# Attention ahead of two MoE layers on one core: causal masks added in VectorE's maximum, softmax denominators inverted by way of DRAM, the preparation of k and q spread over two pairs

## The chip, the cores and the metric

One core of one Trainium2 chip runs the kernel. The time is the device time of one execution in microseconds (us). The engines are named as in the profile: PE (TensorE), DVE (VectorE), ACT (ScalarE), POOL (GpSimd) and SP (SyncE, which here only issues DMAs).

## What is computed

Attention with a decay and a causal mask, then a layer of eight experts mixed by a normalised gate, then one of eight experts with a single expert a row. The change touches the attention alone:

```python
B, H, S, D = 4, 8, 576, 64
scores = scale * np.matmul(q, k.transpose(0, 1, 3, 2))        # scale = 1/8
decay = cum[:, :, :, None] - cum[:, :, None, :]               # cum = cumsum(log(clip(f, 1e-4, 1)))
scores = np.where(causal, -1000000000.0, scores + decay)      # causal: column > row
scores = scores - np.max(scores, axis=-1, keepdims=True)
attn = np.exp(scores)
attn = attn / (np.sum(attn, axis=-1, keepdims=True) + 1e-09)
out = np.matmul(attn, v)
...
x = _moe_ref(x=x, **moe_kwargs)
return _moe2_ref(x=x, **moe2_kwargs)
```

## The kernel before

The 32 heads are worked off in 16 pairs, p = 0 to 15, a pair being two heads of one batch entry. Everything is float32; a number that PE multiplies at its faster rate is split into a rounded part (float32r) and its remainder, which are laid one under the other in the 128 rows of an operand. The order of every engine's instructions is the order in which the program writes them (a manual schedule): each step is a generator, and `weave` takes steps of several generators by positions between 0 and about 1 of an iteration of the main loop (lines 559 to 608). The table `SCH` (line 27) holds most positions. A pair passes through these steps, in different iterations:

- **load** (237, 240): k and q of pair p + 4 come from DRAM in two DMAs, issued by SP at the end of iteration p; v of pair p + 1 (307) right behind.
- **prep(p + 3)** (309 to 331): DMAs of the decay's row into `ka` (312) and of ones into `qb` (314), a cast of k into `ka` on DVE (318), two copies of q into `qb` (320) on ACT, two of k into `kk` (323) and two of q into `qy` (328) on ACT, and the remainders `kk` and `qy` as two subtractions of 64x1152 on POOL (325, 330). Nine steps between .2 and 1.16 of an iteration; `kk` and `qy` have four buffers each, as `ka` and `qb`.
- **path1(p + 2)** (333 to 373): the maximum of every row of scores, needed before the exponential. PE multiplies q by k in tiles of 128 rows into the two buffers `p1` of PSUM; a mask (identity times a triangle of large negative numbers, `identr` and `maskr`, 282 to 285) is added by a further matmul into the triangle of the diagonal block (344, 357, 366), seven of them a pair. DVE takes the maxima: the first two tiles hold both heads and one reduction (346) serves both; then one tile a head (358), and for the last 64 rows two reductions over 512 columns (360), a small one over the diagonal block (368), and their joining (369). Lines 371 and 372 split the negated maxima into `m20`.
- **mrow(p + 1)** (374 to 382): PE transposes `m20` (378) into a `p1` buffer, ACT copies it (380), and POOL issues the DMA that puts it into two rows of `qb` (381).
- **path2(p)** (384 to 415): scores again, transposed and with decay and maximum inside the product (389, 390), into buffers `p2`; ACT's exponential (401, 412) into `pt`; POOL sets the part above the diagonal to zero (393, 413).
- **attn_v** (417 to 464): `pt` times v, head 0 from .6 of iteration p, head 1 in iteration p + 1 (428). The v operand holds 64 columns of v and 64 of ones, so that 64 rows of the result carry the denominators. ACT reads result and denominators apart, two instructions of 64x576 a head (461, 462).
- **norm** (466 to 482): six reciprocals of 128x96 (471) and one product of 128x576 (474) on DVE, and the store to `xgd` (480), over iterations p + 1 and p + 2.
- **norm_few** (484 to 507) takes the place of norm for p = 13 and p = 15 (`FEW`, 510): ACT reads result and denominators together (452), a DMA lays the 1152 denominators out as 32x36 (453), DVE takes one reciprocal of them (488), a DMA writes them to DRAM (489), two DMAs read them back, each to 64 partitions (493), two products of 64x576 (497) and two to four stores (505) follow.

The MoE stages take the rest of the span; weights and x for them are fetched and prepared from p = 8 on.

## Time and profile before

| | |
|---|---|
| three runs, us | 2044.25, 2044.49, 2046.55 (median 2044.49) |
| the profiled execution, us | 2045.49 |
| its span, us | 2043.8 |
| busy over the span: PE, DVE, ACT, POOL | 98%, 78%, 41%, 12% |
| granted TensorE clock (mean) | .999 |
| instructions | 28069 |

The span is that of the instructions that the profiler recorded; the execution's own time is 1.69 us longer. A busy share over the whole span says little about the attention stage, which is a ninth of it: the views of single stretches and the timelines are the ones to read. PE's matmuls overlap and their ends are modelled, so the time from one start to the next tells what one takes from its stream.

### The profile page before, as it was taken

What the parts mean: (1) busy time and instruction counts of PE and PEld (TensorE: products, weight loads), DVE (VectorE), ACT (ScalarE), POOL (GpSimd) and SP (SyncE); (2) the same over time, 40 slices, a digit from 0 to 9 for tenths busy, and PEclk for the clock granted to TensorE, in tenths of its full rate; (3) what the DMA queues carried; (4) which work ended last, traced back from release to release, by engine and by line L of the source; (5) the groups of instructions that cost most, each with busy time, mean ns of one, the idle gap of its engine ahead of it and who ended that gap; (6) DMA issues with size and microseconds to landing.
All of it is one profiled execution on the core that took longest, in us unless ns stands there. A gap on an engine that the chain in (4) does not pass through costs nothing. (4 is left out here: it accounts for less than half of the span.)

```text
span 2043.8 us, 28069 instructions
## 1 busy us (share of the span) xinstructions
PE 1999.7 (98%) x10257; PEld 1774.6 (87%) x10257; DVE 1594.8 (78%) x3023; ACT 834.4 (41%) x1415; POOL 243.5 (12%) x302
## 2 busy tenths in 40 slices
PE   5999999999999999999999999999999999999998
PEld 4998878889989988998998898889989998888887
DVE  8999888887777787888888788888888876555625
ACT  4888543333333343333333334333333332344524
POOL 6776200000000010000001001000000100022111
PEclk9999999999999999999999999999999999999999
DMA  4555331122113123212222223222112223155424
GB/s 148 177 174 209 111 130 62 62 67 78 62 62 114 62 85 104 88 68 73 78 77 63 93 85 109 79 68 93 68 68 82 69 63 114 68 196 176 157 84 151
DMA packets 58483, 203.01 MB, mean 99 GB/s; under 512 B 20578, under 2 KB 24486, under 8 KB 41948
## 3 DMA queue, kind: packets, MB, share of 16 engines
q1 hardware_dynamic: 53152, 189.52, 27.4%
q0 software_dynamic: 4992, 11.29, 1.6%
q8 instruction: 82, 1.34, 0.3%
q14 instruction: 69, 0.57, 0.1%
q10 hardware_dynamic: 188, 0.28, 0.1%
HBM read 185.93 MB, written 15.86 MB: 99 GB/s over the span
## 5 line engine op out<-in xcount | busy, mean ns | idle before, releaser
L964 PE MATMUL o<-w,H 128*128 128x512 f32 x1152 | 450.3, 391 | 0.0
L962 PE MATMUL o<-w,H 128*128 128x512 f32 x1152 | 450.1, 391 | 0.0
L963 PE MATMUL o<-w,H 128*128 128x512 f32 x1152 | 450.0, 391 | 0.0
L1016 ACT ACTIVATE H<-u 128x384 fp32r<-128x384 f32 x192 | 101.0, 526 | 630.6 <-DVE u L1031 624.3
L964 PEld LDWEIGHTS o<-w,H 128*128 128x128 f32 x1152 | 216.2, 188 | 45.5
L962 PEld LDWEIGHTS o<-w,H 128*128 128x128 f32 x1152 | 216.3, 188 | 42.7
L963 PEld LDWEIGHTS o<-w,H 128*128 128x128 f32 x1152 | 216.2, 188 | 42.2
L995 DVE SCALAR_TENSOR_TENSOR acc<-o,Pt,acc 128x512 f32<-128x512 f32 x252 | 188.4, 748 | 75.3 <-PE o L964 73.8
L943 PE MATMUL C<-xc,wc 128*128 128x384 f32 x1152 | 234.0, 338 | 1.5 <-DVE c L1078 1.3
L943 PE MATMUL B<-xc,wc 128*128 128x384 f32 x1152 | 231.8, 335 | 2.4 <-DVE u L1063 1.4
L943 PE MATMUL A<-xc,wc 128*128 128x384 f32 x1152 | 231.9, 335 | 1.2
L943 PEld LDWEIGHTS C<-xc,wc 128*128 128x128 f32 x1152 | 204.4, 188 | 11.4 <-DVE c L1078 2.1
L943 PEld LDWEIGHTS A<-xc,wc 128*128 128x128 f32 x1152 | 201.9, 188 | 4.6 <-ACT ta L1059 4.5
L943 PEld LDWEIGHTS B<-xc,wc 128*128 128x128 f32 x1152 | 202.1, 188 | 4.1 <-DVE u L1063 2.3
L1020 DVE SCALAR_TENSOR_TENSOR H<-A,H 128x384 fp32r<-128x384 f32 x96 | 53.5, 557 | 108.0 <-ACT H L1016 108.0
L219 DVE TENSOR_TENSOR w<-raw,w 128x512 fp32r<-128x512 f32 x190 | 123.6, 683 | 0.4 <-ACT w L215 0.4
L193 DVE TENSOR_TENSOR wc<-tw,wc 128x512 fp32r<-128x512 f32 x188 | 123.7, 694 | 0.0
L1016 ACT ACTIVATE H<-c 128x384 fp32r<-128x384 f32 x96 | 50.5, 526 | 178.9 <-DVE c L1078 178.9
L943 PE MATMUL D<-xc,wc 128*128 128x384 f32 x576 | 116.0, 335 | 1.0 <-DVE wc L193 1.0
L428 PE MATMUL av<-pt,va 128*128 128x192 f32 (+3 forms) x448 | 109.9, 359 | 1.6 <-DMA va<-in_va_dram 1.6
L1020 DVE SCALAR_TENSOR_TENSOR H<-u,H 128x384 fp32r<-128x384 f32 x192 | 109.9, 572 | 1.3 <-ACT H L1016 1.2
L869 POOL DMA_INDIRECT slots<-pay,sli x18 | 19.4, 1078 | 720.4 <-DVE base L867 357.4
(330 smaller groups left out, 3418.5 us busy)
## 6 DMA issues: line engine op xcount, KB each, us to landing
raw<-in_wa_dram SPq DMA_DIRECT2D x95, 1024.0 KB
kq<-in_kq_dram SPq DMA_DIRECT2D x32, 576.0 KB
raw<-in_wb_dram SPq DMA_DIRECT2D x16, 1024.0 KB
wc<-in_wb_dram SPq DMA_DIRECT2D x16, 1024.0 KB
va<-in_va_dram SPq DMA_DIRECT2D x16, 640.0 KB
xr<-xgd SPq DMA_DIRECT2D x21, 384.0 KB
x1d<-acc SPq DMA_DIRECT2D x18, 256.0 KB
wgb<-in_wg2t_dram SPq DMA_DIRECT2D x16, 256.0 KB
```

Source lines behind the costliest of these rows:

```text
L193: eng.tensor_tensor(wc[:, 1, c], src, wc[:, 0, c].bitcast(F32), op=ALU.subtract)
L219: nc.vector.tensor_tensor(t[:, 1, c], raw[:, c], t[:, 0, c].bitcast(F32), op=ALU.subtract)
L428: PE.matmul(av[:, 256 + i0:256 + i1], vt[:, jt, h, :], rhs, start=start, stop=stop)
L869: POOL.indirect_dma_start(out=slot_list[t % 4], in_=pay[:, t, :], in_offset=None, out_offset=bass.IndirectOffsetOnAxis(ap=sli[:, t:t + 1], ...
L943: PE.matmul(a[:, 0:L], w[wa_][k], x[:, xa_, k], start=(start and k == i == 0), stop=(stop and k == 1 and i == 2), skip_group_check=True)
L962: PE.matmul(o, h[:, 0, ts_], w[:, 0, c], start=(b == 0), stop=False)
L963: PE.matmul(o, h[:, 0, ts_], w[:, 1, c], start=False, stop=False)
L964: PE.matmul(o, h[:, 1, ts_], w[:, 0, c], start=False, stop=(b == 3))
L995: DVE.scalar_tensor_tensor(ac, o, p[e], ac, op0=ALU.mult, op1=ALU.add)
L1016: ACT.activation(h[f_][:, 0, half * L:(half + 1) * L], src, AF.Relu)
L1020: DVE.scalar_tensor_tensor(h[f_][:, 1, c], src, 0.0, h[f_][:, 0, c].bitcast(F32), op0=ALU.max, op1=ALU.subtract)
```

## The change

**Masks.** The seven mask matmuls go, and `identr` and `maskr` with them. A tile `mask` in SBUF holds 384 columns of zeros and then the triangle (128 columns); a slice of it is added in the same DVE instruction that takes the maximum (sum and maximum, in place on PSUM, with an accumulator that a second instruction reads out). Each such maximum covers one head, so there are ten a pair in place of eight reductions and a joining; the last two take the maximum over the 512 columns before as their start.

**Denominators.** `norm_few` serves every pair but p = 14. A pair's reciprocal and write stand at the start of iteration p + 2, the broadcasts near its .38, the products and stores from .66. The broadcast of a head goes into the half of the other head's result tile that holds spent denominators. `rx`, `r`, `x` and `den` have three buffers; the DRAM tiles are 16.

**Preparation and loads.** `prep(p + 3)` makes its first two steps (the cast, the copies to `qb`, the DMAs) between .5 and .8 of iteration p, and its other seven (copies to `kk` and `qy`, POOL's subtractions) between .02 and .75 of iteration p + 1. `kk` and `qy` have three buffers instead of four. The load of k and q stands at .82 to .88 in the iteration, that of v at .64 to .7.

```diff
-        kk_, qy_ = (... bufs=NQ) for _ in range(NQ)] ...)
+        kk_, qy_ = (... bufs=NK) for _ in range(NK)] ...)
...
+            def top(out, src, rows, m, first=LOWEST):
+                DVE.tensor_tensor_reduce(src, src, mask[0:rows, m], 1.0, first, ALU.add, ALU.max, out)
...
                 for h in range(2):
-                    PE.matmul(a3[:, h], qb_[:, h, n - P:n], ka_[:, h, 0:n], start=(h == 0), stop=False, ...)
-                PE.matmul(a3[:, :, n - P:n], identr, maskr.unsqueeze(1).to_broadcast([P, 2, P]), ...)
-                DVE.tensor_reduce(mx.rearrange("p (h i) -> p h i", h=2)[:, :, it], a3, axis=AX.X, op=ALU.max)
+                    PE.matmul(a3[:, h], qb_[:, h, n - P:n], ka_[:, h, 0:n], start=(h == 0), stop=(h == 1), ...)
+                for h in range(2):
+                    top(mx[:, 5 * h + it:5 * h + it + 1], a3[:, h], P, slice(512 - n, 512))
...
                     if it < 4:
-                        PE.matmul(a[:, i0:jl], identr, maskr, start=False, stop=True)
-                        DVE.tensor_reduce(mx[:, col:col + 1], a[:, :jl], axis=AX.X, op=ALU.max)
+                        top(mx[:, col:col + 1], a[:, :jl], P, slice(512 - jl, 512))
...
-            PE.matmul(a[:, 0:128].rearrange(...), identr, maskr[:, 0:64].unsqueeze(1).to_broadcast([P, 2, 64]), ...)
-            DVE.tensor_reduce(mo[:, 2:4], a[:64, 0:128].rearrange("p (h j) -> p h j", h=2), axis=AX.X, op=ALU.max)
-            DVE.tensor_tensor(mx[0:64].rearrange("p (h i) -> p h i", h=2)[:, :, 4], mo[:, 0:2], mo[:, 2:4], op=ALU.max)
+            for h in range(2):
+                top(mx[0:64, 5 * h + 4:5 * h + 5], a[:64, 64 * h:64 * h + 64], 64, slice(384, 448), mo[:, h:h + 1])
...
-            r = mo.rx[:, 2 * S:3 * S] if p == npair - 1 else mo.rk[:, 0]
+            r = [t[f"x{1 - h}"] for h in range(2)]
...
-        FEW = (npair - 3, npair - 1)
+        FEW = [p for p in range(npair) if p != npair - 2]
...
+            elif p > 1:
+                items += [(norms[p - 2], 1, 0.02, 0.08), (norms[p - 2], 1, 0.35, 0.41), (norms.pop(p - 2), 3, 0.66, 0.9)]
...
+            if p + 4 < npair:
+                items.append((iter_kq(p + 4), 1, 0.82, 0.88))
+            if p + 1 < npair:
+                items.append((iter_v(p + 1), 1, 0.64, 0.7))
...
+            if p and p + 2 < npair:
+                items.append((late, 7, 0.02, 0.75))
             if p + 3 < npair:
-                items.append((prep(p + 3), 9, *(SCH["pr"] if p else (0.5, 1.0))))
+                late = prep(p + 3)
+                items.append((late, 2, 0.5, 0.8))
             weave(*items)
-            if p + 4 < npair:
-                load(p + 4)
-            if p + 1 < npair:
-                load_v(p + 1)
```

How the order of instructions moves, at two places. First DVE where a pair's row maxima have just been split and the next pair's begin (`p_...` are PSUM tiles, `mx_...` the maxima, `m_...` the split ones). Before:

```order
L371 TENSOR_SCALAR m_1160<-mx_119 128x10
L372 SCALAR_TENSOR_TENSOR m_1160<-mx_119,m_1160 128x10
L471 RECIPROCAL r<-r 128x96 x2
L346 TENSOR_REDUCE mx_118<-p_1177 128x2
L346 TENSOR_REDUCE mx_118<-p_1193 128x2
L318 CAST ka_113<-kq 64x2x576
L358 TENSOR_REDUCE mx_118<-p_1210 128x1
L358 TENSOR_REDUCE mx_118<-p_1228 128x1
```

Now:

```order
L371 TENSOR_SCALAR m_845<-mx_131 128x10
L372 SCALAR_TENSOR_TENSOR m_845<-mx_131,m_845 128x10
L488 RECIPROCAL den<-den 32x36
L341 ISA p_856,mx_130<-p_856,mask 128x128
L341 ISA mx_130 128x1
L341 ISA p_856,mx_130<-p_856,mask 128x128
L341 ISA mx_130 128x1
L341 ISA p_873,mx_130<-p_873,mask 128x256
L341 ISA mx_130 128x1
L341 ISA p_873,mx_130<-p_873,mask 128x256
L341 ISA mx_130 128x1
L341 ISA p_887,mx_130<-p_887,mask 128x384
```

Two reciprocals of 128x96 ahead of the maxima have become one of 32x36, the two double maxima have become four with a read behind each, and the cast has gone from behind them.

Second, PE at the same place, from the second tile of a pair's row maxima to the transposition of the pair before (L378). Before:

```order
L343 MATMUL p_897<-ka_114,qb_110 128x256 x2
L344 MATMUL p_897<-maskr,identr 128x2x128
L389 MATMUL p_906<-qy,kk 128x320
L390 MATMUL p_906<-qb_108,ka_112 128x320
L389 MATMUL p_906<-qy,kk 128x192
L390 MATMUL p_906<-qb_108,ka_112 128x192
L428 MATMUL av_876<-pt,va 128x192
L355 MATMUL p_914<-ka_114,qb_110 128x384
L357 MATMUL p_914<-maskr,identr 128x128
L378 MATMUL p_918<-cs,m_864 20x128
L389 MATMUL p_923<-qy,kk 128x192
L390 MATMUL p_923<-qb_108,ka_112 128x192
```

Now:

```order
L348 MATMUL p_873<-ka_126,qb_122 128x256 x2
L389 MATMUL p_878<-qy,kk 128x320
L390 MATMUL p_878<-qb_120,ka_124 128x320
L389 MATMUL p_878<-qy,kk 128x192
L390 MATMUL p_878<-qb_120,ka_124 128x192
L428 MATMUL av_848<-pt,va 128x192
L358 MATMUL p_887<-ka_126,qb_122 128x384
L378 MATMUL p_890<-cs,m_845 20x128
L389 MATMUL p_895<-qy,kk 128x192
```

The two mask matmuls are gone from the stretch (L344, L357); the transposition follows the third tile's product directly, in the buffer that the second tile held.

## Rows read from the trace of the kernel before

**Rows 1.** Busy time by stretch: start:end, length, PE, PEld, DVE, ACT, POOL, PEclk, DMA, GB/s.

```profile
43.05:57.36 14.31, 14.31 (x88) 13.27 (x88) 12.00 (x18) 10.18 (x18) 11.99 (x14) 1.00 0.54 180
57.36:69.28 11.92, 11.92 (x82) 11.01 (x82) 10.38 (x19) 10.43 (x18) 9.30 (x15) 1.00 0.42 154
119.67:131.59 11.92, 11.92 (x82) 11.01 (x80) 11.23 (x21) 10.44 (x19) 8.78 (x12) 1.00 0.52 184
176.00:204.00 28.00, 26.70 (x177) 23.95 (x176) 25.31 (x47) 22.82 (x40) 19.30 (x29) 1.00 0.49 169
```

**Rows 2.** Timeline of PE at a pair's start: start, length, line, operation.

```profile
124.25 0.33 PE L344 MATMUL p<-maskr,identr 128*128 128x256 f32 x1
124.42 0.28 PE L389 MATMUL p<-qy,kk 128*128 128x256 f32 x1
...
125.31 0.53 PE L343 MATMUL p<-ka,qb 128*128 128x256 f32 x2
125.68 0.28 PE L344 MATMUL p<-maskr,identr 128*128 128x256 f32 x1
125.80 0.30 PE L389 MATMUL p<-qy,kk 128*128 128x320 f32 x1
...
126.81 0.22 PE L357 MATMUL p<-maskr,identr 128*128 128x128 f32 x1
126.87 0.27 PE L378 MATMUL p<-cs,m 128*20 128x128 f32 x1
```

**Rows 3.** DVE's groups, attention stage (34 to 236): busy us, mean ns | idle before.

```profile
L471 DVE RECIPROCAL r<-r 128x96 f32<-128x96 f32 x84 | 59.5, 726 | 0.0
...
L358 DVE TENSOR_REDUCE mx<-p 128x1 f32<-128x512 f32 x30 | 19.5, 651 | 1.4 <-PE p L357 1.4
...
L358 DVE TENSOR_REDUCE mx<-p 128x1 f32<-128x384 f32 x29 | 14.8, 540 | 0.8 <-PE p L357 0.7
...
L474 DVE TENSOR_TENSOR x<-x,r 128x576 f32<-128x576 f32 x13 | 9.0, 690 | 0.0
```

**Rows 4.** Timeline of DVE, same pair.

```profile
123.26 0.22 DVE L368 TENSOR_REDUCE mo<-p 64x2 f32<-64x128 f32 x1
123.51 0.63 DVE L369 TENSOR_TENSOR mx<-mo 64x2 f32<-64x2 f32 x1
...
125.75 0.95 DVE L346 TENSOR_REDUCE mx<-p 128x2 f32<-128x256 f32 x2
126.62 1.51 DVE L318 CAST ka<-kq 64x1152 fp32r<-64x1152 f32 x1
```

**Rows 5.** Timeline of POOL, same pair.

```profile
121.49 2.64 POOL L325 TENSOR_TENSOR kk<-kq,kk 64x1152 fp32r<-64x1152 f32 x1
...
124.87 2.65 POOL L330 TENSOR_TENSOR qy<-kq,qy 64x1152 fp32r<-64x1152 f32 x1 [0.36 <-ACT qy L328]
```

**Rows 6.** DVE's groups over the whole run.

```profile
L801 DVE CUSTOM_DVE_ANT_0 dump<-acc,wgb 128x512 f32<-128x512 f32 x96 | 65.6, 684 | 6.1 <-DMA wgb<-in_wg2t_dram 6.1
...
L1031 DVE TENSOR_TENSOR u<-C,u 128x384 f32<-128x384 f32 x96 | 53.2, 554 | 19.5 <-PE C L943 19.4
...
L801 DVE DVE_READ_ACCUMULATOR2_ANT lg<- 128x1 f32 x96 | 7.9, 83 | 0.0
```

**Rows 7.** Single lines: shortest/median/longest ns, first and last start us.

```profile
L318 DVE CAST ka<-kq x16: 751/1511/4043, 14.8 to 187.3; 64x1152 fp32r<-64x1152 f32 x16
...
L369 DVE TENSOR_TENSOR mx<-mo x16: 153/636/1530, 29.5 to 209.4; 64x2 f32<-64x2 f32 x16
...
L488 DVE RECIPROCAL den<-den x1: 357/357/357, 221.2 to 221.2; 32x36 f32<-32x36 f32 x1
...
L493 SPq DMA_DIRECT2D kq<-rden x2: 488/538/589, 222.9 to 223.5; - x2
...
L497 DVE TENSOR_TENSOR r<-r,kq x1: 840/840/840, 227.4 to 227.4; 64x576 f32<-64x576 f32 x1
```

More of the change, by code (lines that the diff above doesn't have):

```diff
@@ L64, in tile_attn_moe_moe2 @@
     xgd = [dram.tile([KD, P, TG * P], F32, name=f"xgd{g}") for g in range(NG)]
-    rd = [dram.tile([2, S], F32, name=f"rden{i}") for i in range(2)]
+    rd = [dram.tile([2, S], F32, name=f"rden{i}") for i in range(B * NP)]
     sm = ctx.enter_context(tc.tile_pool(name="sm", bufs=1))
@@ L241, in load_kq @@
             return t
-        kk_, qy_ = ([sb.tile([P, 2, w], F32R, name=n, bufs=NQ) for _ in range(NQ)] for n, w in (("kk", SI), ("qy", S)))
+        kk_, qy_ = ([sb.tile([P, 2, w], F32R, name=n, bufs=NK) for _ in range(NK)] for n, w in (("kk", SI), ("qy", S)))
         qb = [sb.tile([P, 2, SI], F32R, name=f"qb_{i}", tag=f"qb_{i}", bufs=1) for i in range(NQ)]
@@ L265, in clear @@
                 POOL.memset(t[0:64, :, S:SI].bitcast(F32), 0.0)
-            POOL.memset(kk_[i][:, :, S:SI].bitcast(F32), 0.0)
+            if i < NK:
+                POOL.memset(kk_[i][:, :, S:SI].bitcast(F32), 0.0)
         pattern(POOL, one[:, 0:1280], 4)
@@ L281, in attention @@
             POOL.memset(p4_[i], 0.0)
-        identr = sb.tile([P, P], F32R, name="identr", bufs=1)
-        POOL.tensor_copy(identr, ident)
-        maskr = sb.tile([P, P], F32R, name="maskr", bufs=1)
-        POOL.tensor_copy(maskr, cmask)
+        mask = sb.tile([P, 512], F32, name="mask", bufs=1)
+        POOL.memset(mask[:, 0:384], 0.0)
+        POOL.tensor_copy(mask[:, 384:512], cmask)
         clear(1)
@@ L456, in attn_v @@
             if h == 0:
-                t["r"] = sb.tile([P, S], F32, name="r", bufs=2)
-                t["x"] = sb.tile([P, S], F32, name="x", bufs=2)
+                t["r"] = sb.tile([P, S], F32, name="r", bufs=3)
+                t["x"] = sb.tile([P, S], F32, name="x", bufs=3)
             o = slice(64 * h, 64 * h + 64)
@@ L486, in norm_few @@
             b, hp = divmod(p, NP)
-            u = FEW.index(p)
+            u = p
             DVE.reciprocal(t["den"], t["den"])
@@ L496, in norm_few @@
                 o = slice(64 * h, 64 * h + 64)
-                DVE.tensor_tensor(t[f"x{h}"][o], t[f"x{h}"][o], r[o], op=ALU.mult)
+                DVE.tensor_tensor(t[f"x{h}"][o], t[f"x{h}"][o], r[h][o], op=ALU.mult)
                 yield
@@ L518, in first_weights, with iter_kq, iter_v @@
             yield from mo.sums_w(0, r, tmp, wc, DVE)
+        def iter_kq(p):
+            load(p)
+            yield
+        def iter_v(p):
+            load_v(p)
+            yield
         def chain(*gens):
@@ L588, in attention @@
             if p == npair - 2:
-                mo.rk = sb.tile([P, 1, S], F32, name="kq", bufs=2)
                 items.append((fw, 3, *SCH["w0"]))
```

46 lines of the change are left out of this document (21 added, 25 removed).

## The prediction, made before the changed kernel had run

> **What bounds the kernel now.** I read first how long each engine is busy in single stretches [rows 1]. The change touches only the attention stage, about the first 236 us of the span; it goes through 16 pairs of heads, and in each pair PE multiplies, ACT takes exponentials, DVE takes maxima and divides, POOL cuts triangles and subtracts. Two stretches that are one pair long each, 62 us apart, both last 11.92 us. DVE is busy 10.38 us in the one and 11.23 in the other, POOL 9.30 and 8.78; PE is busy all 11.92 in both. A period that stays the same while DVE's sum moves by .85 us isn't DVE's, though DVE has little room. So in the middle pairs **PE sets the period**, and an edit is worth what it takes off PE's stream, so long as nobody makes PE wait. The first pair (14.31 us) and the stretch from 176 to 204 us are different: PE still fills the first, but POOL has 11.99 us of work there, and later PE is idle 1.3 us of 28.
>
> Then PE's timeline [rows 2], where starts tell more than durations, since matmuls overlap: from a mask matmul's start to the next start is what it takes from the stream. Then DVE's groups and timeline [rows 3, 4] beside POOL's [rows 5], for what DVE must do more, and when.
>
> **1. The mask matmuls go.** By starts [rows 2]: the two of 256 columns take .17 (124.25 to 124.42) and .12 us (125.68 to 125.80), each of four of 128 columns .06 (126.81 to 126.87), and the one at a pair's end, of 128 columns in two pieces, I put at no more than .12. The sum is .29 + .24 + .12 = .65; the stream won't close up quite without a gap, so I take **.6 us a pair**.
>
> **2. DVE: what it gets and loses.** Lost for a pair [rows 3, 4]: six reciprocals (6 x .726 = 4.36), their product (.69), the two double maxima (.95), two maxima of 512 and two of 384 columns (1.30 + 1.08), the small maximum (.22) and its joining (.63): 9.2, and about 8.4 once the overlaps of neighbours come off. Gained: ten masked maxima. The trace has no such instruction on PSUM; the nearest rows [rows 6] are the 128x512 custom product with its accumulator read (.684 + .083), and a 128x384 sum of a PSUM and an SBUF tile (.554). The line through the two gives .42 for 256 columns, .29 for 128 and .23 for 64, so twice (.68 + .55 + .42 + .29 + .23) = 4.35, less ten overlaps of .08: 3.55. Ten reads add 0 to 1.6 (.8 taken, at .083), and second maxima of a shared tile that wait for the first some .4. One small reciprocal (.36) [rows 7] and two products of 64 rows (.75 each taken, between the .84 of the one shown [rows 7] and the .69 of 128 rows [rows 3]) make it **6.6**; the ends are 5.4 (no reads, no waits) and 7.9 (reads of .16 and twice the waits). DVE's work falls by 1.8 at the likeliest, .5 at the worst. As PE sets the period this is worth nothing by itself; it is what keeps the dearer maxima off the path. The cover gone, each .1 us of DVE above PE's period would cost 1.3 us in all.
>
> **3. What is given back.** The place is the start of a pair, where PE's transposition of the maxima (L378) takes the p1 buffer that the second tile before it held. In the timeline the two double maxima run from 125.75 to 126.70 [rows 4], and the transposition starts at 126.87 [rows 2]: .17 of slack. The masked maxima of those two tiles are four instructions instead of two: 2 x (.29 + .083) less an overlap = .67 for the first tile, 2 x (.42 + .083) less one = .93 for the second. Count in today's times, with the masks ahead of it (.17 + .12 + .06) gone: the transposition is due at 126.52, and the second tile's matmuls, which end at 125.84 now, at 125.67. If DVE comes to that tile at once, .93 later is 126.6, a wait of .1; if it starts on the two tiles as late as today, at 125.75 + .67 + .93 less an overlap = 127.27, a wait of .75. DVE has less to do ahead of it, so it will come earlier, but not by all of that: I take **.3 a pair**, with .1 and .75 as ends.
>
> The Trainium skill ("VectorE: DVE Perf Modes", section "The DRAIN you can't avoid") says that an operation doesn't start until the one before has left the pipeline, and so speaks against splitting one maximum into two. The trace shows some overlap: the pair of maxima runs to 126.70 and the cast after it starts at 126.62. By the rule alone four maxima would hold the tile some .3 longer, the whole .6 would go back, and the sum would be no change.
>
> **4. POOL's subtractions and DVE.** A DVE operation with two SBUF operands, or a cast, waits until a POOL subtraction has ended: the tiny joining of 64x2 started at 123.51 and ended at 124.14, when the subtraction begun at 121.49 ended (124.13); its shortest run is .153 [rows 4, 5, 7]. The cast begun at 126.62 ended at 128.13, behind the subtraction that ends at 127.52, against .751 at its shortest. A maximum with one operand, inside the first subtraction, took its usual .22. Two products of 64 rows now stand where one stood, and POOL subtracts in .44 of a pair's time (2 x 2.65 of 11.92): the pair's stall there lies between 0 and 2.65; by the change's positions they fall into the later subtraction, so 2.0 is taken. So DVE has 11.23 less stalls of .48 and .76 = 10.0 of its own now, 8.2 after, and with the cast's stall (.6) and the products' (2.0) 10.8: under PE's 11.3 (11.92 - .6). Hidden, but barely.
>
> **5. The denominators' way.** Reciprocal, write, two broadcasts and 2 to 4 half stores a pair on SP. The one pair that does it now has the reciprocal at 221.2, broadcasts issued at 222.9 and 223.5, and the products at 227.4 [rows 7]; that is 4.5 us from first broadcast to product, waits and order included. The change leaves from .38 to .7 of a period, 3.8 us, and DVE must wait if the data is late, with the maxima queued behind. Between no wait and .7 us a pair I take none: that pair's products weren't shown to wait for the transfer. One ACT read of 128 rows replaces two of 64: less work on an engine that has 1.5 us to spare [rows 1]. Moving the casts and copies over two pairs and the loads ahead by a fifth of a period changes no count; POOL keeps the same two subtractions. I cost these at nothing, PE's full stream being the cover. The last two pairs keep their way.
>
> **6. The start.** The first 20 maxima stand ahead of PE in the first pairs without cover: +1.2 to +1.6 us. Against that the first pair's stretch is freed of two POOL subtractions' share and four ACT copies that move a pair later: -1 to -2. Net 0, ends -2 and +2.
>
> **The sum.** (.6 - .3) x 13 pairs in the middle = -3.9 us; start and end 0. The profiled execution took 2045.49 us (span 2043.8), 1.0 above the median of the runs, 2044.49; taken off the median the forecast is **2040.6 us**, on its own terms 2037 to 2043.5 (.5 to .1 us a pair, with a part of the start's ends).
>
> **The rivals.**
> *All of PE's gain stays* and more: the maxima come early, the period falls to 11.3 (-7.8), the start gives 1.2 and the late pairs, where PE is idle 1.3 us [rows 1], another 1.5 of DVE's relief: 2034. For it: DVE's falling sum. Against: the .17 of slack at the transposition.
> *All given back*: the wait there is .6 to .75 a pair (0 to +2 in all) and the start dear by up to 1.5: 2045 to 2047, taken as 2046, no change (2043 to 2049). For it: DVE has no idle time ahead of those two maxima [rows 4]; it comes to them late, behind reciprocals.
> *Slower, the masked maxima are held by POOL as the joining was.* They read the mask from SBUF. Then DVE's held kind is maxima 4.7 + products 1.5 + cast .75 = 7.0, to be laid end to end with POOL's 5.3 [rows 5]: 12.3, or 13.3 where half of DVE's other 2 us falls outside; 12.8 is .9 over today, 11.7 in all: 2056 (2050 to 2063). It decides once DVE's sum passes 11.92. Against: the other operand is in PSUM, and a maximum of one PSUM operand ran freely [rows 4].
> The Trainium skill ("SBUF — State Buffer", section "Who interferes with whom") says that a vector operation with at most one SBUF input doesn't contend with GpSimd, and one with two does; the trace agrees for the .22 maximum and for the joining, and no row has a PSUM and an SBUF input beside a subtraction. By it this rival falls away.
> *Slower, the broadcasts come late*: .5 us of DVE wait over its spare .6 in most pairs, +6: 2050. Transfers are busy half the time [rows 1], and a kq load now starts nearer to them.
> *The change doesn't do what it says* only in that p = 14 keeps its reciprocals; this moves nothing.
>
> **How the numbers follow.** Forecast .38, all kept .24, all given back .23, held by POOL .10, late broadcasts .05. 0.2% is 4.1 us: faster means under 2040.4, slower over 2048.6. Faster: half of the forecast's own range lies there (.19), and all of "all kept" (.24): .43. Slower: the held maxima .10, the broadcasts .05, and a quarter of "given back" .06: .21. Same: .36. The range from 2032 to 2050 takes in the first three cases with their ends and leaves out the held maxima and part of the broadcasts and of the best.
>
> **What would show it.** The pair's period, first: near 11.6, with PE still busy in all of it. The transposition waiting for DVE's second maxima by some .3. The 128x512 masked maximum near .68 with a read of about .08; if it is twice that where POOL subtracts, the POOL rival is right. Products longer than .75 beside a subtraction. DVE's sum per pair near 10.8; if it falls to 9 and the period to 11.3, all is kept. A period unchanged at 11.9 with PE idle at one place a pair is the second rival; DVE idle in front of the products on a transfer is the fourth. I am wrong if the period moves while PE's work does not, that is if PE was not the bound.

## The result, and the profile after

The changed kernel is slower: the median of its four runs is 2057.16 us (2053.16 to 2059.17) against 2044.37 before, a ratio of 1.0059 with a 95% interval of 1.0040 to 1.0078. The forecast was 2040.6 us, its range 2032 to 2050: the time is 16.6 over the forecast and outside the range. The profiled execution took 2053.16 us with a span of 2051.5, 7.7 more than before's 2043.8.

```profile
PE 1997.4 (97%) x10145; PEld 1760.9 (86%) x10145; DVE 1572.1 (77%) x3163; ACT 812.4 (40%) x1389; POOL 254.3 (12%) x301
```

The page's busy times don't tell where the loss is. The starts of the transposition L378 do: there is one a pair, and from one to the next is a pair's **period**. Number the 15 periods of the attention stage from the first. From the PE timelines of before and after, in us:

```
                before   after
first L378       30.15   24.31
periods 1 to 2   25.20   24.04
period 3         11.91   11.43
periods 4 to 11  95.36   99.75   (11.92 and 12.47 each in the mean)
period 12        11.93   16.23
period 13        13.05   16.71
period 14        13.05   16.54
period 15        10.99   12.36
rest of span   1832.16 1830.13
```

So the start gave 5.84 us and the end 2.03, periods 1 to 3 another 1.64; periods 4 to 11 took 4.39, and the last four 12.82 (4.30, 3.66, 3.49, 1.37). The sum is +7.7. The medians differ by 12.8; the profiled execution is the fastest of its four, and the rest isn't in these periods. In a second profile of the same program (e18 below, 2057.23 us, near the median) the first transposition starts 3.96 later and periods 4 to 11 are the same 12.46, so some 4 us of the rest lie in the start.

The busy times by stretch, whose columns are those of [rows 1], for periods 3, 5, 12 and 13:

```profile
48.35:59.78 11.43, 11.33 (x74) 10.11 (x75) 7.65 (x27) 8.69 (x17) 8.44 (x12) 1.00 0.41 139
72.62:85.08 12.46, 11.84 (x73) 10.12 (x74) 10.27 (x29) 8.68 (x16) 9.25 (x13) 1.00 0.62 191
159.53:175.76 16.23, 12.79 (x74) 11.13 (x75) 8.83 (x28) 8.68 (x16) 8.28 (x12) 0.91 0.69 243
175.76:192.47 16.71, 13.58 (x74) 11.71 (x73) 12.34 (x30) 9.28 (x17) 9.31 (x12) 0.88 0.59 199
```

In period 3 no products are due yet, and PE's stream without masks takes 11.43 us, .49 less than before. From period 4 on it is 12.46: PE is idle .6 us, though DVE has only 10.27 us of work. Period 12 is 4.8 longer than period 3 and DVE has *less* to do in it than in period 5: something is waited for.

DVE's groups of the attention stage (34 to 246 us); they answer to [rows 3, 6, 7]:

```profile
L341 DVE CUSTOM_DVE_ANT_0 p<-p,mask 128x512 f32<-128x512 f32 x28 | 19.4, 692 | 4.2 <-PE p L358 4.1
...
L497 DVE TENSOR_TENSOR r<-r,x 64x576 f32<-64x576 f32 x14 | 18.6, 1326 | 10.5 <-DMA x<-rden 9.2 <-DMA r<-rden 1.2
L341 DVE CUSTOM_DVE_ANT_0 p<-p,mask 128x384 f32<-128x384 f32 x28 | 16.0, 576 | 13.4 <-PE p L358 13.4
L341 DVE DVE_READ_ACCUMULATOR2_ANT mx<- 128x1 f32 x112 | 15.6, 139 | 0.0
...
L115 DVE TENSOR_TENSOR xc<-xr,xc 128x768 fp32r<-128x768 f32 x7 | 11.5, 1642 | 7.0 <-ACT xc L114 6.9
...
L497 DVE TENSOR_TENSOR x<-x,r 64x576 f32<-64x576 f32 x14 | 10.6, 756 | 0.4
```

The masked maxima cost what was taken for them (.692 and .576 against .68 and .55), the reads .139 instead of .083. But the first of the two products takes 1326 ns in the mean where the second, of the same size, takes 756, and DVE stands 10.5 us ahead of it for the broadcasts. The remainder of x (L115) takes 1642 in the mean.

DVE's timeline in period 5 (start, length, line, operation, idle time before):

```profile
74.17 0.57 DVE L341 CUSTOM_DVE_ANT_0 p<-p,mask 128x384 f32<-128x384 f32 x1 [1.09 <-PE p L358]
...
75.07 0.70 DVE L341 CUSTOM_DVE_ANT_0 p<-p,mask 128x512 f32<-128x512 f32 x1 [0.27 <-PE p L358]
...
77.70 0.68 DVE L362 TENSOR_REDUCE mo<-p 64x1 f32<-64x512 f32 x1 [0.49 <-PE p L358]
78.31 2.11 DVE L497 TENSOR_TENSOR r<-r,x 64x576 f32<-64x576 f32 x1
80.35 0.67 DVE L362 TENSOR_REDUCE mo<-p 64x1 f32<-64x512 f32 x1
81.06 0.76 DVE L497 TENSOR_TENSOR x<-x,r 64x576 f32<-64x576 f32 x1
81.85 0.28 DVE L341 CUSTOM_DVE_ANT_0 p<-p,mask,mo 64x64 f32<-64x64 f32 x1
...
82.64 0.17 DVE L371 TENSOR_SCALAR m<-mx 128x10 fp32r<-128x10 f32 x1
...
83.37 0.30 DVE L341 CUSTOM_DVE_ANT_0 p<-p,mask 128x128 f32<-128x128 f32 x1
...
84.53 0.43 DVE L341 CUSTOM_DVE_ANT_0 p<-p,mask 128x256 f32<-128x256 f32 x1
84.88 0.14 DVE L341 DVE_READ_ACCUMULATOR2_ANT mx<- 128x1 f32 x1
```

POOL's timeline, same pair, and then PE's:

```profile
72.42 2.65 POOL L326 TENSOR_TENSOR kk<-kq,kk 64x1152 fp32r<-64x1152 f32 x1
...
77.18 2.63 POOL L331 TENSOR_TENSOR qy<-kq,qy 64x1152 fp32r<-64x1152 f32 x1
```

```profile
85.08 0.28 PE L378 MATMUL p<-cs,m 128*20 128x128 f32 x1 [0.47 <-DVE mx L341]
```

The product begun at 78.31 ends at 80.42, .6 after the subtraction of 77.18 (79.81), nearly as if it had begun there: it is **held**. A masked maximum at 74.17, inside the subtraction of 72.42, took its usual .57. DVE waits for PE three times before the hold (1.09, .27, .49) and never after it: the last maxima, the scaling into `m20`, and the first four maxima of the next pair run back to back until the transposition, which waits .47. A product free of the hold takes about .74, so this one is 1.37 late, and the period is 1.03 over 11.43; in period 4 the hold is 2.57, 1.83 over, and the period 1.41 over. About .4 us a pair is **slack** (time that a delay may take without making the pair longer), the rest is paid.

The last pairs differ. SP's queue (start, length of the issuing, transfer), DVE, POOL and PE there:

```profile
158.74 4.24 SPq L102 DMA_DIRECT2D xr<-xgd  x4
163.03 0.43 SPq L489 DMA_DIRECT2D rden<-den  x1
167.28 0.48 SPq L493 DMA_DIRECT2D x<-rden  x1
```

```profile
170.19 0.75 DVE L497 TENSOR_TENSOR r<-r,x 64x576 f32<-64x576 f32 x1 [4.90 <-DMA x<-rden]
...
180.79 3.27 DVE L115 TENSOR_TENSOR xc<-xr,xc 128x768 fp32r<-128x768 f32 x1 [1.52 <-ACT xc L114]
```

```profile
180.61 2.64 POOL L331 TENSOR_TENSOR qy<-kq,qy 64x1152 fp32r<-64x1152 f32 x1
```

```profile
171.81 0.41 PE L348 MATMUL p<-ka,qb 128*128 128x128 f32 x2 [3.44 <-DMA qb<-slots]
```

In period 12 SP issues four loads of x in 4.24 us, then the write of the reciprocals, and the broadcasts 4.25 us behind the write, once that has landed; the product stands 4.90 us for them. The 4.25 is not peculiar to this pair, for from write to broadcast the other middle pairs take 1.5 to 5.1; what is peculiar is that the write is issued 5.1 us after its reciprocal has ended (157.93), behind the loads. Behind the broadcasts in the same queue is the row of ones for `qb`, and PE waits 3.44 for that. Without the row of ones PE would have begun hardly earlier: the buffer of its tile comes free only at 171.55, when the maximum behind the late product has ended. What follows shows in the busy times of the end of period 12 and the start of 13:

```profile
168.37:171.81 3.44, 0.00 (x1) 0.03 (x1) 1.58 (x3) 0.00 (x0) 0.00 (x0) 1.00 0.38 107
171.81:175.76 3.95, 3.95 (x20) 3.52 (x21) 3.33 (x16) 1.76 (x3) 0.65 (x3) 0.65 0.87 317
175.76:182.00 6.24, 6.24 (x40) 5.75 (x39) 3.22 (x7) 5.37 (x11) 5.80 (x8) 0.95 0.42 146
```

After PE has done nothing for 3.44 us its granted clock is .65 (part of the time at 1.2 GHz) for the next 3.95 us, and near full again after that. The idle time and .35 of 3.95 make 4.82, and period 12 is 4.80 over 11.43. In period 13 the remainder of x starts .18 us after a subtraction and takes 3.27 (.95 unheld); in period 14 another takes 3.44.

Three theories were put to the test, two out of these lines and one (B) my own term of the transposition's buffer. **A, held by POOL**: an operation of DVE with two SBUF operands (product, remainder of x) stands behind a subtraction on the stretch from the last tile to the next transposition, where no slack is. **B, the buffer**: four maxima instead of two keep the `p1` tile from the transposition. **C, late broadcasts**: SP's order delays the reciprocals' way.

### The profile page after: what moved, and what is told of

Same layout as the page of the kernel before. It is cut to its first block, busy times and chain, and to the rows that moved or that the text cites. A ratio compares the mean times of both kernels' runs of the same rounds, so it can differ in the third digit from the quotient of the medians.

```text
span 2051.5 us, 28162 instructions
## 1 busy us (share of the span) xinstructions
PE 1997.4 (97%) x10145; PEld 1760.9 (86%) x10145; DVE 1572.1 (77%) x3163; ACT 812.4 (40%) x1389; POOL 254.3 (12%) x301
## 5 line engine op out<-in xcount | busy, mean ns | idle before, releaser
L955 PEld LDWEIGHTS C<-xc,wc 128*128 128x128 f32 x1152 | 204.4, 188 | 11.3 <-DVE c L1090 2.1
```

Source lines behind the costliest of these rows:

```text
L955: PE.matmul(a[:, 0:L], w[wa_][k], x[:, xa_, k], start=(start and k == i == 0), stop=(stop and k == 1 and i == 2), skip_group_check=True)
```

## The experiments

Where the expectations speak of "pair 10" and the two after it, periods 12, 13 and 14 are meant.

What all of them gave: the median of 5 to 12 runs in us (4 for before and changed) and the 95% interval of the ratio to before's runs on the same chip beside it; then from each one's profile the start of the first transposition, the mean of periods 4 to 11, and the last four:

```
                          median   ratio             first  4 to 11  period 12  13    14    15
before                    2044.37                    30.15  11.92    11.93 13.05 13.05 10.99
changed                   2057.16  1.0040 to 1.0078  24.31  12.47    16.23 16.71 16.54 12.36
e18 changed, once more    2058.20  1.0052 to 1.0079  28.27  12.46    15.24 17.69 15.27 12.94
e6  no subtractions       2040.11  .9966 to .9985    23.58  11.83    16.98 12.93 12.71 12.76
e7  masks only            2044.82  .9993 to 1.0011   30.66  12.42    12.19 13.75 13.59 10.55
e3  masks back on PE      2063.08  1.0077 to 1.0104  27.86  12.55    18.82 16.59 16.65 12.81
e5  products later        2053.51  1.0031 to 1.0065  24.31  12.37    18.45 16.61 16.48 10.98
e1  subtractions earlier  2057.46  1.0047 to 1.0075  30.52  12.95    15.48 14.95 14.28 13.89
e17 transposition apart   2056.52  1.0048 to 1.0081  24.26  12.49    17.88 16.15 16.56 12.65
e2  x loaded later        2060.71  1.0066 to 1.0094  28.17  12.47    17.20 16.79 16.54 12.35
e14 reciprocal earlier    2056.73  1.0048 to 1.0072  30.48  12.44    17.69 16.52 16.57 12.52
e11 broadcasts by ACT     2076.67  1.0142 to 1.0170  28.16  13.80    14.69 21.62 17.03 12.35
e8  three moves           2048.59  1.0000 to 1.0021  30.49  12.44    16.07 13.04 12.19 11.69
e9  five moves            2052.02  1.0020 to 1.0038  24.60  12.81    14.11 14.12 12.06 13.75
e10 five, start too       2051.01  1.0015 to 1.0035  25.32  12.89    12.71 16.50 12.56 12.80
e12 five, by ACT          2078.10  1.0128 to 1.0161  30.44  13.83    16.65 15.97 15.37 13.48
e13 halves                2053.01  1.0023 to 1.0050  28.16  12.44    16.38 14.67 14.10 12.08
e15 e13, e14, x spread    2043.63  .9984 to 1.0002   28.16  12.13    12.11 12.44 12.24 14.34
e16 e15, other order      2036.36  .9945 to .9970    25.04  12.04    11.44 12.70 12.71 12.87
```

**e18** is the changed kernel unaltered.

> The changed kernel unaltered, once more: its middle periods again 12.3 to 12.5, pair 10 16 us, the next two 16 to 17, by all theories; the first transposition somewhere between 24 and 31 us, and the time between 2053 and 2060 with it.

The first transposition comes anywhere from 23.6 to 30.7 us, 24.31 and 28.27 in two executions of the changed kernel itself. Single times differ by as much, so the periods say more than one time. The last pairs differ too. Period 14 of changed, then of e18:

```profile
192.47:209.01 16.54, 13.23 (x73) 11.44 (x74) 12.39 (x30) 9.30 (x18) 9.37 (x12) 0.90 0.32 87
```

```profile
196.68:211.95 15.27, 11.61 (x73) 10.12 (x73) 12.23 (x30) 9.32 (x18) 9.65 (x13) 1.00 0.29 82
```

PE waits 3.21 us in the one and 3.22 in the other, behind a remainder of x that is held for 3.44 in both. The granted clock is .90 and 1.00. So of the 3.49 by which period 14 is over before's, some 1.3 are the clock and 2.2 the hold.

**e6, no subtractions**: POOL's two instructions are dropped from the changed kernel, so the remainders of k and q stay the rounded copies.

```
-            POOL.tensor_tensor(kk[64:128, :, 0:S], ...)
-            POOL.tensor_tensor(qy[0:64], ...)
```

> The changed kernel without POOL's two subtractions of 64x1152 a pair, so that the remainders of k and q stay the rounded copies (part of the computation left out); nothing else is moved. Theory A: no DVE operation is held, the product takes .75 us, the two x remainders near 1 us, middle periods 11.4 to 11.7. Theory B: middle periods stay at 12.2 or more. Theory C: as pairs get faster the broadcasts (some 7.5 us from reciprocal to product) set them instead: DVE waits on the transfer in front of the product and the periods lie between 11.6 and 12.2, irregular; pair 10 keeps its 16 us.

```profile
68.03:79.48 11.45, 11.33 (x73) 10.12 (x74) 8.98 (x29) 8.70 (x17) 3.11 (x10) 1.00 0.60 207
```

Period 5 (the columns of the stretches above) falls to 11.45, DVE's sum from 10.27 to 8.98, the products take .75, and the transposition doesn't wait, with all of the masked maxima still there. Periods 13 and 14 fall from 16.6 to 12.8. Period 12 stays at 16.98, and of the middle ones those are long (up to 12.51) in which DVE waits for a broadcast (up to 1.40). So the subtractions are what the middle and periods 13 and 14 pay for, as A says, and C holds for period 12.

**e7, masks only**: before, with the changed kernel's masked maxima (and, for room, its list of zeros laid in the mask's own zeros).

```
-                PE.matmul(a3[:, :, n - P:n], identr, maskr...)
-                DVE.tensor_reduce(mx...[:, :, it], a3, axis=AX.X, op=ALU.max)
+                for h in range(2):
+                    top(mx[:, 5 * h + it:5 * h + it + 1], a3[:, h], P, slice(512 - n, 512))
```

> The kernel before with the masked maxima alone: no mask matmuls, reciprocals and preparation as before. DVE loses 3.7 us of maxima a pair and gains 5.4 (ten at 3.5, ten reads at .14, four waits at .1): 12.9 busy against PE's 11.3 and today's period of 11.92. If masked maxima need the denominators' change as cover: middle periods 12.7 to 13.2, 10 to 17 us slower than before. If the masked maxima fit into DVE's slack: 11.9 or less and no slower.

No difference that can be told. Most middle periods are 12.19 here, with DVE busy 11.35 to 11.63 us, and the transposition waits .46 or .47: with six reciprocals a pair DVE comes late, and PE's .49 is given back and .3 more, though no large operation is held there. This profile was the slowest of its ten runs (2050.21); what made the median no worse than before's is open. Much worse was expected: that was a miss.

**e3, masks back on PE** (`identr` and `maskr` and the seven mask matmuls as before), the rest changed.

> The changed kernel with the mask matmuls and the plain maxima of before, all else of the change kept. Theory B (masked maxima are what costs): the wait at the transposition goes, the middle pairs fall from 12.42 to 11.9 us (PE's stream with masks), 4 to 6 us faster. Theory A: DVE has about 1 us less to do a pair, but the product stays held for 2 us and PE gets .6 us more a pair; the middle pairs stay between 12.2 and 12.8 us and the time within 4 us of the changed kernel.

Period 5, and in it DVE's product:

```profile
76.91:88.88 11.97, 11.97 (x83) 10.94 (x81) 9.34 (x16) 8.90 (x17) 8.93 (x12) 1.00 0.63 210
```

```profile
82.95 2.38 DVE L499 TENSOR_TENSOR r<-r,x 64x576 f32<-64x576 f32 x1
```

Periods 4 to 7 are 11.96 to 11.99, nearly before's 11.92, and theory A had expected 12.2 to 12.8: a miss. The product is held here too, 1.6 us, and PE is never idle. PE's stream is .5 longer with the masks, and ahead of the transposition stand two maxima instead of four, so the delay still fits. The hold costs a middle pair something only together with the masked maxima, and e6 shows the converse: four maxima without a hold cost nothing. From period 8 on it is 12.6 to 13.7, where DVE waits 2.0 to 3.3 ahead of the product, in two of four for a broadcast by the profile, and period 12 is 18.82. So the other half of the change does harm without the masks' help, through C from period 8 on and, in periods 13 and 14, through a held remainder of x (3.26) and a held cast (3.18).

**e5, products later; e1, subtractions earlier.**

```
e5 -(norms.pop(p - 2), 3, 0.66, 0.9)   +(norms.pop(p - 2), 3, 0.84, 1.08)
e1 -(late, 7, 0.02, 0.75)              +(late, 7, 0.02, 0.52)
```

> The changed kernel with the products and their stores at .84 to 1.08 of an iteration instead of .66 to .9: behind POOL's second subtraction, and with 2 us more for the broadcasts. Periods are from one transposition (L378) to the next, since the start itself differs by up to 6 us between runs. Theory A (a DVE operation held by a subtraction sends its delay round a loop of DVE's maxima, PE, ACT and POOL): product near .75 us, middle periods 11.4 to 11.8 instead of 12.3 to 12.5. Theory B (the transposition's buffer): still 12.2 or more, with the wait of .47 in front of L378. Theory C (late broadcasts): the 4.9 us wait in pair 10 shrinks by 2 us or more.

> The changed kernel with the other seven steps of the preparation between .02 and .52 of an iteration instead of .02 and .75, so that POOL's second subtraction begins some 1.7 us earlier, ahead of DVE's products. Theory A (the products of two SBUF operands, and the x remainder of 128x768 in two late pairs, are held by that subtraction, and the maxima queued behind them come late): the first product falls from 2.1 to 2.6 us to about .75, the middle pairs from 12.42 to 11.9 us or less (4 us or more over eight pairs), the two x remainders from 3.3 us to about 1 (4 to 5 us more): 8 us faster than the changed kernel. Theory B (four masked maxima instead of two hold the PSUM buffer that the transposition wants, .47 us a pair): products fall too, but the middle pairs stay at 12.3 to 12.5 and the time within 5 us. Theory C (broadcasts late behind other loads): the 4.9 us wait in pair 10 stays.

Later products make most middle periods 12.2 instead of 12.4; theory A had expected 11.4 to 11.8, another miss. In a period of 12.19, DVE's two products and then PE's transposition:

```profile
93.07 0.74 DVE L497 TENSOR_TENSOR r<-r,x 64x576 f32<-64x576 f32 x1
93.84 0.76 DVE L497 TENSOR_TENSOR x<-x,r 64x576 f32<-64x576 f32 x1
```

```profile
96.60 0.28 PE L378 MATMUL p<-cs,m 128*20 128x128 f32 x1 [0.46 <-DVE mx L341]
```

Nothing is held on the stretch, but the products now stand behind the scaling into `m20`, after DVE's last wait for PE, and the pair is .76 over 11.43. So what decides is what stands on that stretch, held or not.

Earlier subtractions make them 12.95, dearer than changed. DVE's timeline of e1, then POOL's:

```profile
109.14 3.52 DVE L319 CAST ka<-kq 64x1152 fp32r<-64x1152 f32 x1
...
113.80 0.74 DVE L497 TENSOR_TENSOR r<-r,x 64x576 f32<-64x576 f32 x1
```

```profile
109.38 2.66 POOL L331 TENSOR_TENSOR qy<-kq,qy 64x1152 fp32r<-64x1152 f32 x1
```

The product is free, and the cast is held in its place: 3.52 where .75 is its length. It starts .24 us ahead of the subtraction, and is held all the same, while the subtraction takes its usual 2.66. A hold that is moved isn't removed.

**e17, transposition apart**: it takes a tile of `p2` instead of `p1`, for B.

```
-            a = ps.tile([P, 512], F32, name="p1", bufs=2)
+            a = ps.tile([P, 512], F32, name="p2", bufs=2)
```

> The changed kernel with one edit: the transposition of the maxima takes a PSUM buffer of path2's pair (p2) instead of one of path1's (p1), so that it no longer waits for the maxima of the tile two before. Theory B: the .47 us wait at L378 and the .7 us before its weights go, and with them .4 us or more of each middle period: 12.42 falls to 12.0 or less, 4 us faster over all. Theory A: the wait is only where DVE's delay by the hold is paid; it moves to the next matmul that needs a p1 buffer, and the middle periods stay within .15 us of 12.42.

The wait of .47 is gone, .16 stands ahead of a score tile instead, the middle periods are 12.2 to 12.6 but for one of 13.47, and the time doesn't move. The buffer is where the delay shows, not where it comes from.

**e2, x loaded later** (`mo.load_x(0, 0)` at .42 of its iteration instead of at its start); **e14, reciprocal earlier** (it and its write at .8 of iteration p + 1, the broadcasts at .1 of the next: `+(norms[p - 1], 1, 0.8, 0.81)`).

> The changed kernel with the four loads of x (1.5 MB) in iteration 10 issued at .43 of it, behind the broadcasts, instead of at its start. Theory C (the denominators' write stands behind 4.2 us of issues of those loads and behind their data): DVE's wait of 4.9 us ahead of pair 10's product vanishes, the period of 16.2 us there falls to about 12.4, and the time by about 4 us. Theory A and B: if DVE waited for something else there, the period stays at 16 us and the time unchanged.

> The changed kernel with the denominators' chain begun a quarter of an iteration earlier: reciprocal and write at .8 of the iteration before, ahead of the load of k and q on SP's queue, broadcasts at .1, products where they were. Theory C by itself: DVE's waits for broadcasts (10.4 us) go, pair 10 falls from 16.2 to 13 or less; middle periods stay at 12.2 to 12.5 since POOL still holds the product (theory A), the next two pairs at 16 to 17. About 4 us faster. If pair 10 stays above 15 us, the transfers of the preparation, not the denominators', make it late.

Neither cures C alone. In e2 PE waits 3.52 for the row of ones instead; in e14 the product waits 5.77, since the four loads of x still stand ahead of the broadcasts in SP's queue.

**The write and the broadcasts issued by ACT**, alone (**e11**), and with the moves of e9 (**e12**).

```
-            SP.dma_start(rd[u]...)
+            (ACT if p < npair - 2 else SP).dma_start(rd[u]...)
```

> The changed kernel with one edit: the denominators' write and the two broadcasts of pairs 0 to 13 are issued on ACT's DMA queue instead of SP's, so that they don't stand behind the loads of k, q, v and x on one queue. Theory C (the transfer's way through SP's queue is late in pair 10): write to broadcast takes 2 us or less instead of 3.5 to 4.2, DVE's wait of 4.9 us in pair 10 goes, its period falls from 16.2 to about 12.5; the middle periods stay at 12.3 to 12.5 by theory A (the product is still held), the next two at 16 to 17 by theory A. About 4 us faster. If ACT's queue shares the delay (the engines' load, not the queue, is late): pair 10 stays above 15.

> The reordered kernel without collisions, with the denominators' write and broadcasts on ACT's queue and the preparation's two DMAs at .1 of the iteration, behind that write. By theories A and C together nothing of the measured waits is left: no product over .85 us, DVE's wait for broadcasts under 2 us in all, middle periods 11.4 to 11.7, pair 10 and the next two 11.5 to 13.2, time 2032 to 2041 by the luck of the start. If the middle periods stay at 12.2 or more, the transposition's buffer (theory B) or something not named sets them.

The dearest of all. ACT's timeline in e12:

```profile
105.44 0.31 ACTq L491 DMA_DIRECT2D rden<-den  x1
105.79 1.26 ACT L326 ACTIVATE kk<-kq 128x576 fp32r<-128x576 f32 x2 [2.02 <-DVE mx L343]
```

The write must wait for DVE's reciprocal, and ACT's copies and exponentials wait with it: 2.02 us a pair. DVE's waits for broadcasts are gone there. That fits SP's queue as their cause but doesn't show it, since pairs that are 1.4 us longer give the broadcasts more time too. ACT is the wrong place to move them.

**Several moves at once.** **e8**: the products of e5, x loaded in two parts, its first remainders at .1 (`+*((0.1, 0.12) if XS[p] == 1 else (0.2, 0.9))`). **e9**: subtractions .02 to .52, products .72 to .92, the cast at .8, the loads of x one an iteration at .42, remainders at .1 (`+items += [(late, 1, 0.0, 0.02), (late, 2, 0.8, 1.0)]`). **e10**: e9, with the prologue's first generator run behind ACT's copies (`run(g0)` moved).

> The changed kernel with three moves: products at .84 to 1.08; the four loads of x split over iterations 10 and 11 and issued behind the broadcasts; the first two x remainders at .11 of iterations 11 and 12 instead of .55, ahead of POOL's subtractions. If theories A and C together are the cause: middle periods 11.4 to 11.8, the three late periods of 16 to 17 us fall to 12 to 13.5, and the time to 2036 to 2046, at least level with the kernel before. If the late periods have another cause, they stay above 15 us and the time above 2050.

> The changed kernel reordered so that no DVE operation of two SBUF operands and no cast stands where POOL subtracts: the other steps of the preparation at .02 to .52, products at .72 to .92, the cast behind them at .8 to 1; the preparation's two DMAs issued at the start of the iteration; x's four loads one an iteration from 7 to 10; the first two x remainders at .11. Periods from one transposition to the next. Theory A with C (holds, and transfers on which DVE and PE now wait): no product over .85 us, middle periods 11.4 to 11.9, pair 10 below 13 instead of 16.2, 12 to 13 in the next two, time between 2032 and 2044 by the luck of the start. Theory B (the transposition's buffer, with no hold needed): middle periods 12.2. If pair 10 still takes 15 us or more, it isn't the load of x that delays the transfers there.

> The kernel of the run before with one more move in the prologue: ACT's copies of pair 0's k and q, and with them POOL's two subtractions, come behind the copies of the ones pattern, so that DVE's first four casts run before POOL subtracts. If the first transposition's scatter (24.3 to 30.5 us so far) is a race of those casts with the subtractions: it comes at 23 to 26 us in the profile, and the repeated times lie within 3 us of one another, at the lower end of the run before's. If not: the scatter stays 5 us or more.

e8 takes periods 13 and 14 to 13.04 and 12.19. As e5 alone leaves them at 16.61 and 16.48, this is the other moves' doing: the first remainders, at .1, take .96 and .88 there. e9 and e10 lose in the middle what they gain late: most periods are near 12.3, and one in e9 is 15.71, where DVE waits 2.63 for a broadcast. The prologue's order changed nothing that can be told from its scatter.

**Halves.** Each subtraction is cut into two of 64x576 with ACT's copies between them, so that none holds DVE for more than half as long (**e13**); with that, the earlier reciprocal of e14, the loads of x one an iteration at .2, and the remainders at .62 (**e15**); and e15 with the halves in another order, kk's second head first, so that none should run while `m20` is scaled, and the cast at .55 (**e16**).

```
e13 -items.append((late, 7, 0.02, 0.75))
    +items += [(late, 1, at, at) for at in (0.0, 0.02, 0.06, 0.2, 0.22, 0.28, 0.36, 0.56)]
e16 +items += [(late, 1, at, at) for at in (0.0, 0.01, 0.16, 0.2, 0.21, 0.28, 0.33)]
```

> The changed kernel with POOL's two subtractions of 64x1152 cut into four of 64x576 and put into the stretches in which DVE takes maxima alone (at .02, .2, .28 and .56 of an iteration, each with its copy on ACT ahead); the cast, the products, the transfers stay where the change has them. Theory A by itself: no product over .85 us where its data is there; middle periods 11.4 to 11.9 instead of 12.3 to 12.5 as long as no broadcast is late. Theory C: DVE waits for broadcasts in more pairs than the one of the changed kernel (6 to 12 us in all), pair 10 stays above 15 us, and the two x remainders are still caught in part. Time 2046 to 2053.

> Both edits before together, x's four loads one an iteration from 7 to 10, and the first two x remainders at .63 instead of .55. By theories A and C together: middle periods 11.4 to 11.7, pair 10 12 or less, the next two 12 to 13.2, DVE's waits for transfers under 1 us; time 2031 to 2040, below the kernel before. If it stays above 2044, holds and late transfers are not the whole cause.

> The kernel with all three moves, in which one hold is left: m20's scaling takes 1.15 us instead of .17, held by the first half subtraction. Here that subtraction follows both copies of k (so it starts behind m20), all four come ahead of the cast, the cast stands behind the last masked maximum (.625), the reciprocal at .72. Theory A: m20's scaling back to .17 us, no wait at the transposition, middle periods 11.4 to 11.6 instead of 12.13, time 2033 to 2040. If the periods stay at 12.1 with m20 at .17, then the transposition's buffer by itself (theory B) sets them.

e13 missed in the middle: its products are free (.75), but the scaling into `m20` is held for 1.31, and the periods stay at 12.4 where 11.4 to 11.9 was expected. e15 cures C in period 12, which is 12.11 now that the loads of x are apart (in period 15 DVE still waits 3.98 for a broadcast). But its middle periods are all 12.12 to 12.14. DVE's timeline of e15, then POOL's:

```profile
106.57 0.76 DVE L509 TENSOR_TENSOR r<-r,x 64x576 f32<-64x576 f32 x1
...
110.04 1.15 DVE L383 TENSOR_SCALAR m<-mx 128x10 fp32r<-128x10 f32 x1
```

```profile
109.73 1.42 POOL L327 TENSOR_TENSOR kk<-kq,kk 64x576 fp32r<-64x576 f32 x1 [1.76 <-ACT kk L325]
```

The products are free, and the hold stands at an instruction of 128x10, 1.15 instead of .17, on the same stretch without slack. In e16, DVE's timeline and then POOL's:

```profile
99.57 1.42 DVE L319 CAST ka<-kq 64x1152 fp32r<-64x1152 f32 x1
100.92 0.67 DVE L381 TENSOR_REDUCE mo<-p 64x1 f32<-64x512 f32 x1
101.52 0.78 DVE L516 TENSOR_TENSOR r<-r,x 64x576 f32<-64x576 f32 x1
...
104.80 0.17 DVE L390 TENSOR_SCALAR m<-mx 128x10 fp32r<-128x10 f32 x1
```

```profile
105.23 1.43 POOL L325 TENSOR_TENSOR kk<-kq,kk 64x576 fp32r<-64x576 f32 x1 [2.03 <-issue]
```

The scaling takes .17, the subtraction begins after it, the transposition doesn't wait, and five of the eight middle periods are 11.43 to 11.70. One is 14.31, where DVE still waits .86 for a broadcast and then 2.31 for denominators. At 2036.36 us, 9.4 under before's 2045.76 on the same chip, **e16 beats both kernels**, with all of POOL's work done. In its profiled execution (span 2036.7, 7.1 under before's) the start gives 5.1 us and the end 2.7, while the pair of 14.31 eats what the middle gains: its 15 periods sum to .7 more than before's. The interval of its runs is what shows it faster. Its cast is held too (1.42 above), but ahead of that stretch.

## Why the prediction was wrong

- **The masks go: right.** Forecast .6 a pair, measured .49 (11.43 against 11.92).
- **DVE's sum: near, in part by luck.** Forecast 10.8 with the stalls, measured 10.27. Its own work was .8 over (8.98 without subtractions, against 8.2), the stalls 1.3 under (1.3 against 2.6). The maxima were within .03 but for those of 64 columns (.28 against .23), the reads .06 dearer each.
- **The give-back at the transposition: the wait is .47 where .3 was taken, but four maxima alone don't make it.** It is 0 in e6 and e16, which have the same four, and a hold of 1.6 before two maxima costs .05 in e3. It takes four maxima and a DVE that is late. By the Trainium skill's rule ("VectorE: DVE Perf Modes", section "The DRAIN you can't avoid") they alone would give the whole .6 back; with DVE on time the trace doesn't agree, and they give back nothing (periods of 11.45 and 11.43).
- **POOL's subtractions: this is the step that failed.** "Hidden, but barely" set DVE's sum of 10.8 against PE's 11.3 and stopped there. The stall was named, and its size nearly right (2.0 taken, 1.4 to 1.8 measured). But the sum over a pair says nothing of where in the pair the stall falls. It fell after DVE's last wait for PE, where everything up to the transposition is one chain, so .4 of it was hidden and 1.0 to 1.4 us a pair were paid against the 11.43 that PE needs. That the place decides is seen in e5, where free products on the same stretch cost .76, and in e3, where the hold has room and costs .05. The remainders of x, which I didn't name, paid in the same way in periods 13 and 14, 3.66 and 3.49 us over before (e6 has them .1 and .3 under).
- **Masked maxima held by POOL: wrong, as argued.** The maximum at 74.17 inside a subtraction took .57. That this rival's 2056 came within 1.2 of the measured 2057.16 is chance: the maxima aren't held, and DVE's sum in the middle is at most 10.71 (period 4), where it wanted 11.92 passed. The Trainium skill ("SBUF — State Buffer", section "Who interferes with whom") says that whoever starts first keeps the shared ports for its whole instruction. The trace agrees for the product, begun 1.13 behind the subtraction and ended .61 after it, and in e3, where a remainder of x begun .09 ahead of a subtraction takes its usual .96 and the subtraction 3.36. It differs in e1, whose cast began .24 ahead and was held. The page also excepts casts and scalings from the rule of one SBUF input that the prediction took from it, and the scaling into `m20` was held indeed (1.15 in e15).
- **The denominators' way, costed at nothing: wrong in one place.** The rival "broadcasts come late" had .05 and +6 us, spread over most pairs. What came was 4.3 us in period 12 (3.3 in e18), where four loads of x stand ahead in SP's queue, which I hadn't counted, and waits of .2 to 1.4 in the middle. These can cost little where the held product would have ended no sooner: in period 10 DVE waits 1.25 and the product then takes .79.
- **The start: net 0 (-2 to +2) was too narrow.** It gave 5.84 in one profile of the changed kernel, 1.88 in the other. In the one DVE's cast at 10.42 takes .95, ahead of POOL's subtraction of 12.55; in the other it starts at 14.81 and takes 3.17, beside the subtraction of 14.34. Why it goes one way or the other stays open; e10 didn't settle it.

So the sum had the sign wrong because two terms were put at nothing: A, about 1 us a pair and 7 us in periods 13 and 14 (some 1.3 of it the fallen clock), and C, 3.3 to 4.3 us. That A is the larger is shown by e6: in the profiles 5.1 us go with the subtractions in periods 4 to 11 and 7.6 in periods 13 and 14, in the medians 17 of 2057.16.

## What to carry to other kernels

Don't compare an engine's busy sum with the period alone: find its last wait for the bounding engine in a pair, and take every stall and every other piece of work behind that point as paid once the slack there is gone (.4 us here). Where two engines exclude each other, cut the long instruction of the one into pieces and lay them beside instructions of the other that aren't held; moving the whole only chose who is held. The cutting alone bought nothing in the middle (12.44 in e13); the placing did (11.43 to 11.70 in most pairs of e16). A small transfer with a result that someone waits for belongs ahead of large loads in its queue, and not on the queue of an engine that would wait with it. e15 is the evidence for the first, e11 for the second.

## What was not expected of the hardware

- A scaling of 128x10 is held like a product: 1.15 us against .17, beside a subtraction of 64x576.
- An idle time of PE can cost more than itself: after 3.44 us without work the granted clock was .65 for 3.95 us, 1.4 us on top. It needn't: over periods 12 to 14 the clock was .91, .88 and .90 in one profile of the program and 1.00, .81 and 1.00 in the other, which has waits of 2.76, 3.04 and 3.22 us there. The length of the wait alone doesn't decide.
- From the write of the reciprocals to the broadcasts that read it back, SP took 1.5 to 5.1 us in the middle pairs.
- Two executions of one program differ by 4 us (24.31, 28.27) in when their first transposition starts, and by as much in their times (2053.16, 2057.23).
